# Unused tiles of 64 bytes between the pools of a spectral block with an MLP

## The chip, the cores and the metric

The kernel runs on one core of one Trainium2 chip. Times are device microseconds (us) of one execution. TensorE is the matmul engine, VectorE (DVE), ScalarE (ACT) and GpSimd (POOL) compute on tiles in SBUF, the on-chip memory of 128 partitions, and SyncE (SP) issues the DMAs. PSUM holds the results of matmuls. A matmul has two operands in SBUF: the weights, which a weight load brings into the array ahead of it (PEld in the profile), and the moving data, which stream through.

## The reference

One block with adaptive layer norm: a condition vector `c` gives six rows of scale, shift and gate; a spectral filter (a 2-D real FFT over 2048 x 512, a product with a complex weight, and back) is added to x, and then an MLP with Mish.

```
mod = (_silu(c) @ w_mod).reshape(c.shape[0], 6, 1, -1)
h = _layernorm(x) * (1 + ca) + sa
x = x + ga * irfft2(rfft2(h) * (w_r + 1j * w_i))
h = _layernorm(x) * (1 + cb) + sb
x = x + gb * (mish(h @ w1 + b1) @ w2)
```

x has 2048 rows of 512 float32 numbers, w1 is 512 x 1376, w2 1376 x 512.

## The kernel before, in words

The kernel runs in four stages, and in each the program's order is written out by hand, so the order in which an engine gets its work is the order of the calls.

The first stage goes over 16 groups of 128 rows. It does the FFT along the rows (line 206) and, as matrix products, along the columns (lines 251 to 253); the column matrices lie in `mring`, split into a high and a low part of type float32r, and the moving data in work buffers `g1` and `g2`. The second stage goes over 17 groups of frequencies: transpose (line 464), a small transform (line 485), the product with the filter on VectorE, transpose (line 518), a small transform back (line 531). The third goes back along columns (lines 666 and 667, with the matrices `kc`) and rows (line 676, with `kiv`) for the 16 groups. During it the weights w1 and the first parts of w2 are loaded and split.

The fourth is the MLP. It goes over 8 blocks of 256 rows, and in each over 6 items of the hidden dimension, item 0 with the 96 columns that are left over and items 1 to 5 with two tiles of 128. For an item, `up` multiplies by w1: four 512-wide matmuls with the high part `w1h` as weights and both parts of the MLP's input (`h2e` and `h2o`, for blocks of even and odd number) as moving data at line 755, then four 256-wide ones with the low part `w1l` at line 757, for each tile. ScalarE and VectorE make Mish of it (`front`, `back`) and sums of row halves, and `halves` splits the result into activations `ah` and `al` (lines 717 and 718). `down` takes these as weights and w2 as moving data: three passes (high by high, high by low, low by high) for each of seven products of half size, 21 matmuls of 256 columns in an item, at line 808. Item 0 (line 800) and parts of the last block (lines 820 and 823) have 512-wide matmuls instead. `down` of an item stands two items behind its `up`. All these matmuls are float32r, those of stages two and three and line 206 are float32.

Tiles come from pools that are set one behind another in SBUF: `base`, `small`, `work` (the nine work buffers), `big` (the tags `da`, `db`, `cr` and `ci`, each used by several tiles one after another: `mring` and then a part of w2 in `db`, `kc` and then `h2o` in `cr`), then `pw` and `hring` for the first two stages, and in their place `pm` (w1, w2, `h2e`) and `act` (the activations) for the others. A tile's first byte follows from the sizes of all tiles ahead of it. In the built program before, the work buffers, the tiles in `big`, w1, w2, `h2e` and the activations all begin 64 bytes past a multiple of 128; `kiv` begins 32 past one, and `modr` 96.

Of the kernel before, what the change touches and what calls it, by code (L numbers as in the profile page):

```python
# [7 lines left out]
F32 = mybir.dt.float32  # L8
# [4 lines left out]
P = 128  # L13
# [18 lines left out]
def tile_spectral_block(ctx: ExitStack, tc: tile.TileContext, x_d, w1_d, b1_d, w2_d,  # L32
# [4 lines left out]

    base = ctx.enter_context(tc.tile_pool(name="base", bufs=1))
    small = ctx.enter_context(tc.tile_pool(name="small", bufs=4))
    work = ctx.enter_context(tc.tile_pool(name="work", bufs=2))  # L40
    big = ctx.enter_context(tc.tile_pool(name="big", bufs=1))

    dram = ctx.enter_context(tc.tile_pool(name="dram", bufs=1, space=bass.MemoryType.DRAM))
# [555 lines left out]
        apply_gate()  # L599
    first.close()  # L600

    pm = ctx.enter_context(tc.tile_pool(name="pm", bufs=1))
    act = ctx.enter_context(tc.tile_pool(name="act", bufs=2))
    w1h = pm.tile([P, 4, F], F32R, name="w1h")
    w1l = pm.tile([P, 4, F], F32R, name="w1l")
    w2 = {}
    w2[1] = [pm.tile([P, 7, 256], F32R, name=f"w2{i}") for i in range(2)]
    w2hi = pm.tile([P, 7, 256], F32R, name="w2hi")
    w1v = w1_d.rearrange("(k p) f -> p k f", p=P)

    def piece(i):
# [495 lines left out]
```

## Time and profile before

| | us |
|---|---|
| median of 3 runs | 392.77 |
| lowest and highest run | 391.95, 393.06 |
| span of the profiled execution | 390.1 |
| of it TensorE busy | 383.2 |
| VectorE, ScalarE, GpSimd busy | 298.7, 247.3, 96.4 |
| stage of the MLP alone | from 165 on |

The span goes from the first to the last instruction of the profiled execution; what a run takes beside it is start and end. Matmuls overlap each other: the duration of one is longer than the time from its start to the start of the next, so the pace of a run of matmuls is read from starts, and busy time of TensorE near 100% says only that one followed another. PEld rows are weight loads, which run beside the matmul ahead of theirs. A row of a group gives line, engine, operation, tiles written and read, shapes and count, then busy time and mean duration in ns, then the idle time ahead. A row of the chain gives start, length and what ran. A row of waits gives who waited for whom, us in total, how often, and the longest.

### The profile page before, as it was taken

To read this page: it belongs to the slowest core of one execution; us is meant where nothing else is said; L and a number is where in the kernel's file an instruction comes from. 1 tells how busy PE (TensorE), PEld (TensorE's weight loads), DVE (VectorE), ACT (ScalarE), POOL (GpSimd) and SP (SyncE) were. 2 spreads that over 40 slices of the span, in tenths; PEclk is the share of its full clock that TensorE was granted. 3 is DMA by queue.
4 is the path that set the end of the run, shared out by engine and by line. 5 is a ranking of instruction groups with operands and counts; after the bars stand their busy time and mean duration, and the time that the engine had idled before them with its cause. 6 is when DMAs were issued, how large, how long until landed. Compare 5 with 4: busy or idle time off the path is not lost.

```text
span 390.1 us, 7373 instructions
## 1 busy us (share of the span) xinstructions
PE 383.2 (98%) x2744; PEld 355.3 (91%) x2744; DVE 298.7 (77%) x668; ACT 247.3 (63%) x545; POOL 96.4 (25%) x132
## 2 busy tenths in 40 slices
PE   8999999999999999999999999999999999999996
PEld 8899889999999998999999998999999999899984
DVE  1898978876299989887856965965966875987993
ACT  1788756678558647975855765674674674584750
POOL 0677736665077533300000000000000010017000
PEclk9999999999999999999999999999999999999999
DMA  8999994482143410100100100100100200122011
GB/s 262 376 296 343 311 361 141 134 315 55 55 114 87 145 49 28 56 3 0 55 0 3 54 2 0 56 0 2 55 2 0 76 0 2 50 61 106 3 54 54
DMA packets 21315, 36.70 MB, mean 94 GB/s; under 512 B 3840, under 2 KB 6752, under 8 KB 21024
## 3 DMA queue, kind: packets, MB, share of 16 engines
q1 hardware_dynamic: 21280, 36.24, 27.8%
q8 instruction: 21, 0.34, 0.4%
q14 instruction: 14, 0.11, 0.1%
HBM read 32.04 MB, written 4.20 MB: 93 GB/s over the span
## 4 chain that ended last, share of the span: by engine, by line
PE 89%; DVE 5%; ACT 4%; issue 1%; DMA 1%; SPq 0%; DVEq 0%; ACTq 0%
PE bank L808 24%; PE bank L755 20%; PE bank L757 10%; PE bank L485 3%; PE bank L531 3%; PE bank L676 3%; PE bank L206 3%; PE bank L251 3%; PE bank L666 3%; PE bank L667 3%; PE bank L800 2%; PE bank L820 2%; PE bank L645 2%; PE bank L464 2%; PE bank L518 1%; PE bank L262 1%
## 5 line engine op out<-in xcount | busy, mean ns | idle before, releaser
L765 ACT ACTIVATE buf<-bank,b1n 128x256 f32<-128x256 f32 (+1 forms) x88 | 40.8, 472 | 66.4 <-PE bank L757 66.1
L766 DVE TENSOR_TENSOR buf<-buf,bank 128x256 f32<-128x256 f32 (+1 forms) x88 | 35.3, 416 | 38.6 <-ACT buf L765 38.6
L718 DVE TENSOR_TENSOR al<-buf,ah 128x512 fp32r<-128x512 f32 (+2 forms) x85 | 53.7, 655 | 0.7 <-ACT ah L717 0.7
L737 POOL TENSOR_TENSOR buf<-buf,modr 128x512 f32<-128x512 f32 (+1 forms) x3 | 3.9, 1297 | 183.0 <-DMA buf<-in_B_w_dram 175.9
L755 PE MATMUL bank<-h2e,w1h 128*128 128x512 f32 (+1 forms) x176 | 48.4, 397 | 0.0
L755 PE MATMUL bank<-h2o,w1h 128*128 128x512 f32 (+1 forms) x176 | 48.3, 396 | 0.0
L717 ACT CAST ah<-buf 128x512 fp32r<-128x512 f32 (+2 forms) x85 | 43.0, 548 | 1.2 <-DVE buf L782 1.2
L782 DVE TENSOR_TENSOR buf<-buf 128x128 f32<-128x128 f32 x148 | 39.8, 310 | 3.5 <-ACT buf L772 2.2
L772 ACT ACTIVATE buf<-buf 128x512 f32<-128x512 f32 (+1 forms) x48 | 28.6, 596 | 15.3 <-DVE buf L766 15.2
L808 PE MATMUL bank<-w2a,ah 128*128 128x256 f32 x161 | 34.9, 286 | 0.0
L755 PEld LDWEIGHTS bank<-h2o,w1h 128*128 128x128 f32 (+1 forms) x176 | 30.2, 187 | 4.5
L755 PEld LDWEIGHTS bank<-h2e,w1h 128*128 128x128 f32 (+1 forms) x176 | 30.1, 187 | 4.5
L808 PE MATMUL bank<-w2b,ah 128*128 128x256 f32 x147 | 31.8, 283 | 0.0
L757 PEld LDWEIGHTS bank<-h2e,w1l 128*128 128x128 f32 (+1 forms) x176 | 26.7, 185 | 4.2
L757 PEld LDWEIGHTS bank<-h2o,w1l 128*128 128x128 f32 (+1 forms) x176 | 26.7, 185 | 4.2
L757 PE MATMUL bank<-h2e,w1l 128*128 128x256 f32 (+1 forms) x176 | 27.8, 280 | 0.0
L757 PE MATMUL bank<-h2o,w1l 128*128 128x256 f32 (+1 forms) x176 | 27.8, 280 | 0.0
L808 PEld LDWEIGHTS bank<-w2a,ah 128*128 128x128 f32 x161 | 26.7, 191 | 0.0
L667 PE MATMUL bank<-kc,d 128*128 128x128 f32 x128 | 24.8, 275 | 0.0
L666 PE MATMUL bank<-kc,d 128*128 128x128 f32 x128 | 24.7, 275 | 0.0
L808 PEld LDWEIGHTS bank<-w2b,ah 128*128 128x128 f32 x147 | 24.6, 191 | 0.0
L120 DVE BATCH_NORM_STATS2 st<-x 128x6 f32<-128x512 f32 x32 | 22.0, 688 | 0.4
(224 smaller groups left out, 1001.3 us busy)
## 6 DMA issues: line engine op xcount, KB each, us to landing
buf<-in_B_w_dram SPq DMA_DIRECT2D x20, 256.0 KB, 3.0
x<-in_A_x_dram SPq DMA_DIRECT2D x16, 256.0 KB, 5.1
xring<-in_x_t_dram SPq DMA_DIRECT2D x16, 256.0 KB, 5.1
wm<-in_w_mod_dram SPq DMA_DIRECT2D x16, 256.0 KB, 4.5
out_dram<-x SPq DMA_DIRECT2D x7, 512.0 KB, 2.6
mraw<-in_km_dram SPq DMA_DIRECT2D x16, 128.0 KB, 5.1
wqa<-in_w_q_dram SPq DMA_DIRECT2D x8, 256.0 KB, 4.3
wqb<-in_w_q_dram SPq DMA_DIRECT2D x8, 256.0 KB, 5.8
```

The costliest lines, as they stand in the source:

```text
L120: nc.vector.bn_stats(t, x[:, n, :])
L666: nc.tensor.matmul(o, dj[:, 0:128], kc[0][:, n, :], start=True, stop=False)
L667: nc.tensor.matmul(o, dj[:, 64:192], kc[1][:, n, :], start=False, stop=True)
L717: nc.scalar.copy(h, r)
L718: nc.vector.tensor_tensor(l, r, plain(h), op=ALU.subtract)
L755: nc.tensor.matmul(ps, w1h[:, k, fs], h[:, k], start=(k == 0), stop=False)
L757: nc.tensor.matmul(ps[:, 0:256], w1l[:, k, fs], h[:, k, 0], start=False, stop=(k == 3))
L765: nc.scalar.activation(o, ps[:, 256:], AF.Identity, bias=b1n[:rows, f:f + 1])
L766: nc.vector.tensor_tensor(o, o, ps[:, 0:256], op=ALU.add)
L772: nc.scalar.activation(o, o, AF.Mish)
L782: nc.vector.tensor_tensor(o, p, q, op=op)
L808: nc.tensor.matmul(o, a[p][:, e], w2[t][q][:, r], start=(own and half == 0 and t == 1 and i == 0), stop=(end and i == 2 and (n, half) != ( ...
```

## The change

A helper `shift` opens a pool with one tile of 16 float32 numbers a partition (64 bytes) that nothing writes or reads. It is called ahead of `work`, ahead of `big` and ahead of `pm`, and ahead of `act`, and one such tile stands in `pm` between w1 and w2. The pool `act` is opened after the tiles of `pm` are declared instead of ahead of them. Nothing else is changed: each engine has the same instructions in the same order with the same waits.

```diff
     base = ctx.enter_context(tc.tile_pool(name="base", bufs=1))
     small = ctx.enter_context(tc.tile_pool(name="small", bufs=4))
+
+    def shift(stack):
+        pool = stack.enter_context(tc.tile_pool(name="half_line", bufs=1))
+        pool.tile([P, 16], F32, name="half_line")
+
+    shift(ctx)
     work = ctx.enter_context(tc.tile_pool(name="work", bufs=2))
+    shift(ctx)
     big = ctx.enter_context(tc.tile_pool(name="big", bufs=1))
...
+    shift(ctx)
     pm = ctx.enter_context(tc.tile_pool(name="pm", bufs=1))
-    act = ctx.enter_context(tc.tile_pool(name="act", bufs=2))
     w1h = pm.tile([P, 4, F], F32R, name="w1h")
     w1l = pm.tile([P, 4, F], F32R, name="w1l")
+    pm.tile([P, 16], F32, name="half_line")
     w2 = {}
     w2[1] = [pm.tile([P, 7, 256], F32R, name=f"w2{i}") for i in range(2)]
     w2hi = pm.tile([P, 7, 256], F32R, name="w2hi")
+    shift(ctx)
+    act = ctx.enter_context(tc.tile_pool(name="act", bufs=2))
```

The first byte of the tiles that matter, in a partition, before and after, and what it leaves over a multiple of 128:

| tile | before | after |
|---|---|---|
| first work buffer | 51,520 (64) | 51,584 (0) |
| `mring`, later a part of w2 | 96,576 (64) | 96,704 (64) |
| `kc`, later `h2o` | 121,152 (64) | 121,280 (64) |
| `w1h`, `w1l` | 137,536, 159,552 (64) | 137,728, 159,744 (0) |
| first w2 in `pm` | 181,568 (64) | 181,824 (64) |
| `h2e` | 203,072 (64) | 203,328 (64) |
| `ah`, `al` (first) | 211,264, 218,432 (64) | 211,584, 218,752 (0) |

## The prediction

> **What bounds the kernel now.** The page's first part and its second come first, then the same busy times by stage.
>
> ```profile
> span 390.1 us, 7373 instructions
> PE 383.2 (98%) x2744; PEld 355.3 (91%) x2744; DVE 298.7 (77%) x668; ACT 247.3 (63%) x545; POOL 96.4 (25%) x132
> PEclk9999999999999999999999999999999999999999
> ```
>
> ```profile
> core 0: us, PE busy (x) PEld busy (x) DVE busy (x) ACT busy (x) POOL busy (x), PEclk, DMA share, GB/s
> ...
> 165.00:390.00 225.00, 221.29 (x1489) 202.71 (x1488) 168.19 (x383) 136.15 (x278) 10.66 (x9) 1.00 0.08 28
> ```
>
> TensorE is busy 98% of the span at the full granted clock. From 165 us on only the MLP is left, and there VectorE is busy 168.19 of 225 us, or 75%, ScalarE 61%, and the DMA engines 8%. A busy matmul row may hide waiting, so the next view is what the matmuls waited for. The longest waits of TensorE are these, and the rest are shorter:
>
> ```profile
> PE bank L292 <- DVE b1n L311: 1.1, 1, 1.1
> PE bank L262 <- DMA wmc<-in_w_mod_dram: 0.3, 1, 0.3
> ```
>
> So nothing feeds TensorE late; its own pace sets the end. The chain of waits gives that pace, because in the MLP it holds nothing but runs of matmuls, and each run's length is the time until the next run starts:
>
> ```profile
> 185.63 2.51 PE bank L808 x21
> 188.14 0.93 PE bank L755 x4
> 189.07 0.47 PE bank L757 x4
> 189.54 0.94 PE bank L755 x4
> 190.49 0.47 PE bank L757 x4
> 190.96 0.87 PE bank L645 x8
> 191.83 2.52 PE bank L808 x21
> ```
>
> A 256-wide matmul of line 808 starts every 2.51 us / 21 = 119.5 ns, a 512-wide one of line 755 every 0.93 / 4 to 0.94 / 4 = 234 ns, a 256-wide one of line 757 every 117 ns. These numbers come back block after block (2.51 or 2.52 us for the 21, whatever the other engines do), so what sets them lies in TensorE and in what it reads. The groups by form say the same in another unit: the duration of one matmul is a fixed tail longer than its pace.
>
> ```profile
> L755 PE MATMUL bank<-h2e,w1h 128*128 128x512 f32 x160 | 44.0, 396 | 0.0
> L808 PE MATMUL bank<-w2b,al 128*128 128x256 f32 x49 | 13.9, 283 | 0.0
> L757 PE MATMUL bank<-h2e,w1l 128*128 128x256 f32 x160 | 25.3, 280 | 0.0
> L820 PE MATMUL bank<-w2hi,al 128*128 128x512 f32 x4 | 1.6, 389 | 0.0
> L676 PE MATMUL bank<-kiv,buf 128*128 128x128 f32 x128 | 17.0, 276 | 0.1
> L531 PE MATMUL bank<-kv,buf 128*128 128x128 f32 x126 | 16.8, 276 | 0.2 <-ACT buf L521 0.2
> ```
>
> 283 - 119.5 and 396 - 234 and 280 - 117 all give about 163 ns of tail. With it every other row turns into a pace: line 820, also 512 wide, runs at 389 - 163 = 226 ns, 8 ns faster than line 755 with an equal shape; the float32 matmuls of 128 columns (lines 676 and 531) at 113 ns. Matmuls of one shape thus differ by 3 to 8 ns, always the same way at one place of the program, with no wait. They differ only in which tiles they read and in what went before. That the place in SBUF (the on-chip memory) of the two operands plays a part is a possible reading of this, not one that these rows prove.
>
> **The change part by part.** No engine gains, loses or reorders an instruction, and the same waits stand before the same instructions. The unused tiles hold no data and nobody writes them. What moves is where tiles lie. In the built program before, every tile that an MLP matmul reads, and the work buffers, start at 64 past a multiple of 128 bytes. After it the work buffers (51,520 becomes 51,584), w1h and w1l and the activations ah and al start at a multiple of 128; w2, h2e, h2o, the column matrices and the row matrices keep 64, since they move by 128 or 256. Weights and moving data of a matmul, before at equal place in the 128 bytes, now stand 64 apart at lines 251 to 253, 755, 757, 808, 800, 820 and 823, at 531, and at 485 for later groups. At 666 and 667 (both tiles in the same pool) and 676 (kiv starts at 32) less or nothing changes. So the change does what it says; the question is what the chip makes of it.
>
> The counts: line 808 has 21 matmuls in each of 37 items (7 blocks of 5, and 2 in the last), 777; lines 755 and 757 have 352 each, 251, 252 and 253 have 48 each; 800, 820 and 823 together 84.
>
> No row shows a float32r matmul (the single-pass kind of the MLP) whose operands stand 64 apart, so the cost of a place is bounded from both sides. *The good end.* A 256-wide matmul and a 128-wide float32 one each have a weight load of the same 128 columns to overlap, and the second runs at 113 ns, a price that the first may reach: 777 x 6.5 = 5.1 us at line 808, 352 x 4 = 1.4 us at line 757. If the 512-wide ones lose as much again below the quickest row, 226 - 6.5 = 219.5 ns, line 755 gives 352 x 14.5 = 5.1 us. The 48 of line 251 and the 84 of the last lines at some 10 ns give 1.3 us, lines 252 and 253 at 5 ns 0.5 us: 13.4 us together. *The bad end.* The nearest row for a weight load that the memory slows down is line 518, which takes its weights with a step of 16 bytes:
>
> ```profile
> L518 PEld LDWEIGHTS bank<-ident,buf 128*128 128x128 f32 x63 | 8.8, 205 | 0.0
> L531 PEld LDWEIGHTS bank<-kv,buf 128*128 128x128 f32 x126 | 15.5, 193 | 0.4 <-ACT buf L521 0.4
> L518 PE MATMUL bank<-ident,buf 128*128 128x128 f32 x63 | 10.1, 282 | 0.0
> ```
>
> Its load takes 12 ns more and its matmul 282 - 276 = 6 ns more than line 531. 6 ns on the 1,225 matmuls of 256 columns (777 + 352 + 96) is 7.4 us, and 5 ns on line 755 1.8 us: 9.2 us slower.
>
> *The value taken.* Between these ends I take the nearest rows of equal shape in this kernel: line 808 comes down to the pace of line 757 and line 755 to that of line 820, that is, each shape to a pace it already has somewhere. That is 777 x 3 = 2.3 us and 352 x 7 = 2.5 us; line 757 stays; line 251 as line 755, 48 x 7 = 0.3 us; 253 by 3 ns 0.1 us; the 48 of lines 800 and 823 by 6 ns 0.3 us. The sum is 5.5 us. All of it lies on the chain, because TensorE waits for nothing: the MLP's 225 us would become some 220, with VectorE at 168 / 220 = 76%, so nothing else takes over. Why a gain and not a loss: the paces that are to be explained lie above the quickest row of the same shape at nearly every place where all operands share one place in the 128 bytes, so there is more room below than above. This is a choice, not a proof.
>
> [...]
>
> *The float32 matmuls* of 128 columns (531, 485, 206) are costed at nothing: line 676, whose moving tile stands at 32, and line 531, where both stand at 64, have one duration, 276 ns, and loads of 192 to 193 ns. Were the shift worth 3 ns each way, the 126 and 72 of lines 531 and 485 would move the end by 0.6 us.
>
> *The other engines* read and write the moved buffers too. A change of some per cent there is hidden by the matmuls, which they wait for: ScalarE waits 66.1 us in all for line 757.
>
> ```profile
> ACT buf L765 <- PE bank L757: 66.1, 62, 2.2
> DVE buf L766 <- ACT buf L765: 38.6, 42, 2.3
> ```
>
> Where the cover is thin is the first stage, in which the DMA engines are 97% busy and line 251 shows mean durations of 434 instead of 398 ns; its DMA destinations move by 128 bytes only or not at all, so they keep their place in the 128.
>
> ```profile
> 0.00:46.00 46.00, 44.00 (x304) 40.79 (x305) 34.43 (x96) 30.66 (x72) 26.79 (x42) 1.00 0.97 324
> L251 PE MATMUL bank<-buf,mring 128*128 128x512 f32 x48 | 20.8, 434 | 0.6 <-ACT buf L237 0.3 <-DVE buf L244 0.2
> ```
>
> 1% more in these 46 us would be 0.5 us; I take nothing.
>
> The profiled execution has a span of 390.1 us; the median of the three runs is 392.77, so 2.7 us lie around the span. 390.1 - 5.5 = 384.6 us of span makes 387.3 us.
>
> **The rivals.** *First, the place does not matter* (no change, 392.8 us). For it speaks that lines 676 and 531 agree to the nanosecond although their operands stand differently, and that every 21 of line 808 take 2.51 us although their tiles lie in several places, all at 64. Against it, the spread within equal shapes needs some cause. [...]
>
> *Second, the whole excess goes*: the good end, 13.4 us, 392.8 - 13.4 = 379.4 us. For it: the change sets nearly every large matmul to the same new relation at once, so if the equal place is the one cause, all lines gain together. Against: line 820 is quick with all operands at 64.
>
> *Third, the new relation is the worse one* (slower). [...] Line 808's evenness, 119.5 ns at all 777, says its present relation is stable; line 755's steps over rows of 5,504 bytes, which mix places by multiples of 128, run slower than line 820 without such steps, so a relation other than the equal one can cost. Price: 3 ns on the 1,225 matmuls of 256 columns, 3.7 us, and 5 ns on the 352 of line 755, 1.8 us: 5.5 us, 398.3 us. It decides once the pace of line 808 rises above 120 ns.
>
> **How the numbers follow.** The forecast, 387.3 us with a range of its own of 383 to 391, has a chance of 0.35; the whole excess 0.2; no change 0.2; slower 0.25. A run of this kernel tells 0.3%, or 1.2 us, from no change. Faster by more is then 0.35 + 0.2 = 0.55, within it 0.2, slower 0.25. For the range, the low side reaches below the second rival, to 378 us, and leaves out what goes further (under 0.1); the high side reaches into the third, to 398 us, and leaves out its upper part (0.1).
>
> **What would show it.** Right: in the chain of waits the 21 matmuls of line 808 take 2.45 us (117 ns each) instead of 2.51, the 4 of line 755 0.91, with the number of instructions and TensorE's 98% unchanged. The whole excess: 2.37 us for the 21 and durations of 276 ns. No change: 2.51 and 0.93 to 0.94 again. Slower: 2.58 us or more for the 21. I would be wrong in kind if lines 808 and 755 moved in opposite directions, if the blocks of h2e and h2o (which now start differently to w1: 64 below and 64 above, modulo 512) had different paces, or if a new wait of TensorE appeared, by which the other engines and not the matmul's reads would carry the difference.

## The result and the profile after

The change is faster by less than forecast. The median of 4 runs is 389.87 us (389.21 to 390.44) beside 392.72 us of the kernel before in the same session; the ratio is 0.9927, with a 95% interval of 0.9907 to 0.9948, so 2.9 us, from 2.0 to 3.7. The forecast was 387.3 us, 5.5 us less than before. The profiled execution has a span of 387.8 us, 2.3 us less. The ratios here and below leave out slow executions, of which there was one: 1645.82 us among the first experiment's ten.

```profile
span 387.8 us, 7373 instructions
PE 380.7 (98%) x2744; PEld 353.1 (91%) x2744; DVE 298.9 (77%) x668; ACT 247.2 (64%) x545; POOL 96.3 (25%) x132
```

The instructions, TensorE's 98% and the other engines' busy times are as before. The longest waits of TensorE are these; the lines are numbered 7 to 10 higher than before (line 808 is now 818, 755 is 765, 820 is 830):

```profile
PE bank L299 <- DVE b1n L318: 1.1, 1, 1.1
PE bank L258 <- DVE buf L251: 0.9, 2, 0.7
PEld bank L765 <- DVE buf L776: 0.3, 1, 0.3
```

The first is as before. The second, in the first stage, was 0.2 us before, but it is 0.8 us also in the experiment below that moves the activations alone and leaves that stage as it was. The third is new: in the last block one weight load waits for VectorE, and the matmul behind it starts 0.31 us after the one ahead instead of some 0.23.

So the waits give no gain, and the gain is pace. In the chain of waits of the changed kernel, the same kind of stretch of the MLP that was shown of before:

```profile
185.29 2.48 PE bank L818 x21
187.77 0.93 PE bank L765 x4
188.70 0.47 PE bank L767 x4
189.17 0.93 PE bank L765 x4
190.11 0.48 PE bank L767 x4
190.59 0.87 PE bank L655 x8
191.46 2.48 PE bank L818 x21
193.94 0.91 PE bank L765 x4
```

21 matmuls of the down product take 2.48 us instead of 2.51 or 2.52 (118 ns each instead of 119.5), the four of the up product 0.91 to 0.93 instead of 0.93 to 0.94. The groups by form show the same, and that not every line gained:

```profile
L765 PE MATMUL bank<-h2e,w1h 128*128 128x512 f32 x160 | 43.5, 394 | 0.0
L818 PE MATMUL bank<-w2b,al 128*128 128x256 f32 x49 | 13.7, 280 | 0.0
L818 PEld LDWEIGHTS bank<-w2b,al 128*128 128x128 f32 x49 | 9.2, 188 | 0.0
L830 PE MATMUL bank<-w2hi,al 128*128 128x512 f32 x4 | 1.6, 395 | 0.0
```

Line 765 went from 396 to 394 ns and line 818 from 283 to 280, but the quick line of before, 820, went from 389 to 395 ns. A weight load of the down product is shorter too, 188 ns; before it was

```profile
L808 PEld LDWEIGHTS bank<-w2b,al 128*128 128x128 f32 x49 | 9.4, 192 | 0.0
```

Since both programs have the same matmuls in the same order, the time from each start to the next can be summed by line. Line 808 went from 93.5 to 91.8 us (1.7 us less), 755 from 82.5 to 81.5 (1.0 less), 757 stayed at 41.5 and 41.4, 800 and 820 together went from 18.4 to 18.7 (0.3 more, 0.08 of it the new wait). In the float32 lines 485, 531, 666, 667 and 676 the sums agree to 0.02 us.

The first three stages are one source of noise. The first matmul of line 755 starts, before and after, at

```profile
142.46 1.16 PE L755 MATMUL bank<-h2e,w1h 128*96 128x512 f32 x4
```

```profile
142.68 1.16 PE L765 MATMUL bank<-h2e,w1h 128*96 128x512 f32 x4
```

and in the experiments anywhere from 141.4 to 143.7 us, also where these stages are unchanged. From that start to the end of the span it is 390.1 - 142.5 = 247.6 us before and 387.8 - 142.7 = 245.1 us after. This length, called the MLP's length below, carries the comparisons by single profiles.

### The profile page after: what moved, and what is told of

Same layout as the page of the kernel before. It is cut to its first block, busy times and chain, and to the rows that moved or that the text cites. A ratio compares the mean times of both kernels' runs of the same rounds, so it can differ in the third digit from the quotient of the medians.

```text
span 387.8 us, 7373 instructions
## 1 busy us (share of the span) xinstructions
PE 380.7 (98%) x2744; PEld 353.1 (91%) x2744; DVE 298.9 (77%) x668; ACT 247.2 (64%) x545; POOL 96.3 (25%) x132
## 4 chain that ended last, share of the span: by engine, by line
PE 84%; DVE 5%; DMA 4%; ACT 4%; issue 1%; SPq 0%; DVEq 0%; ACTq 0%
PE bank L818 24%; PE bank L765 20%; PE bank L767 10%; PE bank L492 3%; PE bank L538 3%; PE bank L686 3%; PE bank L677 3%; PE bank L676 3%; PE bank L810 2%; PE bank L830 2%; DMA modr<-scb 2%; PE bank L655 2%; PE bank L471 2%; PE bank L258 2%; PE bank L525 1%
```

## The experiments

Two theories had to be told apart first: that a matmul's pace hangs on how its two operands stand to each other (R), or on where a tile begins by itself (A). In all diffs below, `pad(ctx, n)` opens a pool with one unused tile of n bytes a partition. All are edits of the kernel before, and in all that use `pad` the pool `act` is opened after the tiles of `pm`, as in the change. Runs with no ratio are single executions.

**Both operands moved alike.** One unused tile of 64 bytes ahead of the work buffers, and none after it.

```diff
+    pad(ctx, 64)
     work = ctx.enter_context(tc.tile_pool(name="work", bufs=2))
```

> One unused tile of 64 bytes ahead of the work buffers and none after it: all tiles from there on begin at a multiple of 128 bytes, so weights and moving data stand to each other exactly as before, only the place of both is moved by 64. Theory R (the relation of a matmul's two operands sets the pace): nothing changes, 2.51 us for the 21 matmuls of line 808's run, 0.93 to 0.94 us for the 4 of line 755, 392.7 us in all, within 1. Theory A (a tile that begins at a multiple of 128 is read faster by itself): as the change or better, 2.48 us, 0.92 us, 390 us or less.

Measured: 391.45 us, a ratio of 0.9991 (0.9969 to 1.0013) to before. The MLP's length is 389.3 - 141.7 = 247.6 us, as before, and the chain has the old times:

```profile
191.11 2.51 PE bank L817 x21
193.62 0.93 PE bank L764 x4
194.55 0.47 PE bank L766 x4
195.02 0.94 PE bank L764 x4
```

Where a tile begins by itself changed nothing here. Theory A is out.

**The places exchanged.** Weights at 64 past a multiple of 128, moving data at a multiple of it.

```diff
     work = ctx.enter_context(tc.tile_pool(name="work", bufs=2))
+    pad(ctx, 64)
...
+    pad(ctx, 64)
     pm = ctx.enter_context(tc.tile_pool(name="pm", bufs=1))
...
     w1l = pm.tile([P, 4, F], F32R, name="w1l")
+    pm.tile([P, 16], F32, name="pad")
...
+    pad(ctx, 64)
+    act = ctx.enter_context(tc.tile_pool(name="act", bufs=2))
```

> The change with its places exchanged: work buffers, w1 and activations 64 past a multiple of 128 as before, and w2, the MLP's input and the column matrices at a multiple of 128. Theory R (relation): as the change, 2.47 to 2.48 us for the 21 matmuls of the MLP's down product, 0.92 us for the 4 of the up product, 390 us within 1. Theory A (the weights' own place at a multiple of 128 counts): as before, 2.51 us and 0.93 to 0.94 us, 392.7 us.

Measured: 390.38 us, a ratio of 0.9953 (0.9931 to 0.9975); 2.47 to 2.48 us for the 21 of most items, 0.92 to 0.93 us for the 4, an MLP's length of 388.9 - 143.7 = 245.2 us. That is the change's gain in the MLP (245.1 us) with the places exchanged: it is the relation that counted.

**The activations alone.**

```diff
+    pad(ctx, 64)
+    act = ctx.enter_context(tc.tile_pool(name="act", bufs=2))
```

> Only the activations are moved by 64 bytes, everything else stays as before. If each line's pace hangs on its own two operands: the 21 of the down product in 2.48 us, the 4 of the up product still in 0.93 to 0.94 us, the 512-wide matmuls with activations as weights slower by some 5 ns as in the change, a span of 390.1 - 1.5 = 388.6 us. If the gain came from the work buffers or from w1 through other engines: nothing at the down product, 390.1 us.

Measured: a span of 390.1 us, but with a late start of the MLP; its length is 390.1 - 143.5 = 246.6 us, 1.0 less than before. The chain has the expected times, 2.48 us for the 21, whose operands were moved against each other, and 0.93 to 0.94 us for the 4, whose operands were not:

```profile
192.68 2.48 PE bank L817 x21
195.16 0.93 PE bank L764 x4
196.09 0.47 PE bank L766 x4
196.56 0.94 PE bank L764 x4
```

The span was a miss, 390.1 us for 388.6 expected: the MLP starts 1.0 us later, and it gained 1.0 us instead of 1.5. The 512-wide matmuls with activations as weights lost 6 ns, about as expected: at line 820 the median time from start to start is 227 ns before and 233 here.

**A sweep of the distance.** Work buffers, w1 and activations are moved by n bytes, and a second unused tile after the first two brings all else back to its old place modulo 512. With n = 64 this differs from the change in one thing: in the change, padding adds up so that the activations stand 64 from some w2 tiles and 192 from others (modulo 256), and w1 192 from `h2e` and 64 from `h2o`.

```diff
+    pad(ctx, n)
     work = ctx.enter_context(tc.tile_pool(name="work", bufs=2))
+    pad(ctx, 512 - n)
...
+    pad(ctx, n)
     pm = ctx.enter_context(tc.tile_pool(name="pm", bufs=1))
...
     w1l = pm.tile([P, 4, F], F32R, name="w1l")
+    pm.tile([P, (512 - n) // 4], F32, name="pad")
...
+    pad(ctx, n)
+    act = ctx.enter_context(tc.tile_pool(name="act", bufs=2))
```

> Work buffers, w1 and activations are moved by 64 bytes and every other tile keeps its place modulo 512, so that all pairs stand exactly 64 apart modulo 512; in the change some stand 192 or 64 the other way. If only the place modulo 128 counts: the lines as in the change, 2.47 to 2.48 us for 21 and 0.92 to 0.93 us for 4, a span of 387.8 us within 0.7. If the place modulo 512 counts: other paces than in the change, by 1 ns a matmul or more, above all at those products whose distance differs (w2 in the large tiles).

> The sweep by 64 once more, now timed. If its 113.3 ns a matmul of the down product is what its places give each time: 387.7 us within 0.7, 1.1% under before. If it was the luck of one execution: 113.3 ns in the profile again or not, and a median of 390 us.

> As the sweep by 64, with 128 bytes instead: operands that stood at equal place now stand 128 apart modulo 512. Theory B (only the place modulo 128 counts, two alternating halves of 64 bytes): everything as before, 2.51 us for the 21 of the down product (119.5 ns each), 0.93 to 0.94 us for the 4 of the up product, a span of 390 us within 0.7. Theory M (a longer period): another pace, by 1 ns a matmul or more.

> As the sweep by 64, with 256 bytes: theory B as before, 119.5 ns a matmul of the down product and a span of 390 us within 0.7; theory M another pace.

> As the sweep by 64, with 32 bytes, so that half of each 64-byte piece overlaps. Theory B: between before and the sweep by 64, 113 to 120 ns for a matmul of the down product. Theory M: no statement but that it differs from 119.5 ns.

> As the sweep by 64, with 192 bytes, the distance at which the change puts the activations and the large w2 tiles. If only the place modulo 256 and the footing from the matmuls ahead decide: down products at 113.3 or 117.8 ns a matmul, run by run, and none at 119.5; a span of 386 to 389 us. If 192 is one more kind of place with its own pace, as 128 was (117, 120, 123 ns in turn): another figure in all runs.

| n | 21 of the down product, us | one of them, ns | MLP's length, us |
|---|---|---|---|
| 0 (before) | 2.51 to 2.52 | 119.5 to 120 | 247.6 |
| 32 | 2.48 to 2.50 | 118 | 246.6 |
| 64 | 2.38 to 2.40, but for one of 2.48 and two with a wait inside | 113.3 | 242.5 and 242.3 |
| 128 | 2.49 to 2.52 | 118.5 to 120 | 247.5 |
| 192 | 2.38 or 2.47 | 113.3 or 118 | 243.7 |
| 256 | 2.51 to 2.52 | 119.5 to 120 | 247.9 |

256 gives the paces of 0 again, run for run. 128 does not, although its span, 390.2 us, and its MLP are as long as before: summed by line, 755 takes 81.59 us instead of 82.50, and 757 takes 42.15 instead of 41.48. A group of line 757 (now 767) at 128 and at 256, where it has its old 280 ns:

```profile
L767 PE MATMUL bank<-h2e,w1l 128*128 128x256 f32 x160 | 25.7, 283 | 0.0
...
L767 PE MATMUL bank<-h2e,w1l 128*128 128x256 f32 x160 | 25.3, 280 | 0.0
```

So of the shifts that were run, the one by 256 bytes repeats the paces of none, twice the period that the change was drawn for. At 64 nearly all of the down product falls to 113.3 ns, a pace that no line of its shape kept before (117 to 119.5 ns):

```profile
191.34 2.40 PE bank L818 x21
193.74 0.92 PE bank L765 x4
194.66 0.47 PE bank L767 x4
```

Timed, n = 64 has a median of 386.56 us, quicker than the 387.7 within 0.7 that was expected, and a ratio of 0.9859 (0.9838 to 0.9881) to before. It beats both kernels: the change's interval, 0.9907 to 0.9948, lies above it. At 192 the runs alternate between two paces, 2.38 and 2.47, in one kernel; its span of 385.1 us is below the 386 to 389 expected, since its MLP starts at 141.4:

```profile
190.02 2.38 PE bank L818 x21
...
195.20 2.47 PE bank L818 x21
...
199.06 2.38 PE bank L818 x21
...
204.23 2.47 PE bank L818 x21
```

**Is it the weight load?** The kernel before, with the down product's weights read at one address.

```diff
-                nc.tensor.matmul(o, a[p][:, e], w2[t][q][:, r], ...
+                nc.tensor.matmul(o, a[p][:, e, 0:1].to_broadcast([P, P]), w2[t][q][:, r], ...
```

> The kernel before, with the weights of the 21 down products of an item read as one column of the activations, repeated 128 times: the weight load has the same length and reads one address over and over; the products themselves are other ones, so the MLP's result is not computed. Theory C (the weight load's walk through SBUF collides with the walk of the moving data): the pace leaves 119.5 ns, down to 113 ns or less. Theory F (a float32r matmul has a fixed overhead of 13 ns): 119.5 ns stays, 2.51 us for the 21.

Measured: nothing is moved, yet the 21 take 2.38 to 2.41 us, and the MLP's length is 385.7 - 142.8 = 242.9 us.

```profile
L808 PE MATMUL bank<-w2b,al 128*128 128x256 f32 x49 | 13.5, 276 | 0.0
L808 PEld LDWEIGHTS bank<-w2b,al 128*128 128x128 f32 x49 | 9.2, 188 | 0.0
```

The load still has its 128 columns, and 188 ns (192 before). With one address read in place of 128 columns, the down product's matmuls go from 283 to 276 ns. Theory F's 13 ns are what the paces of lines 808 and 820 before leave as a constant part (2 x 119.5 - 226); 6 to 7 of them are gone here, so as a fixed overhead those are out. Theory C's pace came; that two reads collide is its reading, and no trace shows a collision. (The load brings other values, too, and no run changes the values alone; but the sweep by 64 reaches the same pace, 113.3 ns, with the values unchanged.) Lines 755 and 757 fall as well, from 82.5 to 81.8 us and from 41.5 to 41.3, though their own operands are read as before: here the pace of a line changed with that of its neighbours. What sets the 113.3 ns that are left is open.

**What chooses between 113.3 and 118 ns?** With the activations alone moved, every run of 21 had 118; with work buffers and w1 moved too, 113.3, though the down product's operands stand alike in both. So w1 and the activations were moved without the work buffers (shown against the sweep by 64):

```diff
-    pad(ctx, n)                        # n = 64, around the work buffers
-    pad(ctx, 512 - n)
```

> As the sweep by 64, but the work buffers stay where they are before: w1 and the activations are moved by 64 bytes, all else keeps its place modulo 512. With the activations alone moved, the down product ran at 117.8 ns, with work buffers and w1 moved as well at 113.3. If the matmuls that run ahead (the up product) set the footing on which the two streams start: 113.3 ns, a span of 385.6 us within 0.7. If the work buffers do it, through the engines that read and write them beside TensorE: 117.8 ns, 388.5 us.

Measured: both, and a span of 386.1 us. The MLP's length is 386.1 - 143.1 = 243.0 us.

```profile
185.55 2.38 PE bank L818 x21
...
190.71 0.87 PE bank L655 x8
191.58 2.48 PE bank L818 x21
...
196.86 2.40 PE bank L818 x21
```

Runs that follow the up product have 2.38 to 2.40 us, but for one of 2.53 with a wait inside; the one in each block that follows the transposes of line 655 has 2.47 or 2.48. Those transposes take work buffers as weights, and with the work buffers moved as well they lead, but for one case, into the quick pace (2.40 us, above). So at a distance of 64 or 192 two steady paces occur, 113.3 and 118 ns, and in this layout the one that a run has goes with what ran ahead of it.

It does not settle it alone. The sweep by 64 was profiled in two executions of one program, and the run behind the first block's transposes took, in the one and in the other,

```profile
161.97 2.48 PE bank L818 x21
...
161.90 2.40 PE bank L818 x21
```

Nor does a run always keep its pace. In the first of these executions a weight load in the last block waits,

```profile
360.09 0.30 PEld L818 LDWEIGHTS bank<-w,ah 128*128 128x128 f32 x2 [0.29 <-DVE modr L854]
```

and the matmuls of that run start every 113 ns ahead of the wait and every 118 ns behind it; in the other execution the same load waits 0.16 us, and the pace is 113 ns on both sides. Program and tiles are the same; what made the difference between the two executions is not shown. The change itself has both paces: 4 of its 37 runs of 21 take 2.38 to 2.40 us, the others 2.47 or 2.48.

**A layout drawn by this reading.** The sweep by 64 with w1's rows padded, so that the up product's steps over rows no longer mix distances.

```diff
-    w1h = pm.tile([P, 4, F], F32R, name="w1h")
-    w1l = pm.tile([P, 4, F], F32R, name="w1l")
+    w1h = pm.tile([P, 4, 1408], F32R, name="w1h")
+    pm.tile([P, 16], F32, name="pad1")
+    w1l = pm.tile([P, 4, 1408], F32R, name="w1l")
...
-            w2[0] = [w[:, 5376:5888], w2["lo"]]
+            w2[0] = [w[:, 5392:5904], w2["lo"]]
```

> The sweep by 64 with the rows of w1 padded from 5,504 to 5,632 bytes, so that all four steps of the up product stand alike modulo 256; the high part of w1 at equal place with the MLP's input, the low part 64 apart; w2's last part of 96 rows moved by 64, to equal place with the activations. If the place modulo 256 of one matmul's load and stream sets its pace, with 226.7 ns for 512 columns at equal place and 113.3 ns for 256 columns at 64 apart: line 755 goes to 226.7 ns (from 230, 1.1 us in all), line 757 to 113.3 ns (from 116, 0.9 us), the 512-wide matmuls of item 0 from 232 to 227 ns (0.2 us), 385.5 us within 1. If the footing of the matmuls ahead decides as much as the place: one of these stays off, and the down product may fall back to 117.8 ns, 389 us.

Measured: 390.2 us, a ratio of 0.9941 (0.9923 to 0.996), worse than the sweep by 64. The second expectation held in kind. Summed by line, 755 takes 81.8 us (81.35 in the sweep) and 757 41.6 (41.1); only the 512-wide matmuls of item 0 gained, 0.1 us instead of the 0.2 expected. And most runs of the down product fell back:

```profile
186.11 2.48 PE bank L819 x21
...
192.26 2.40 PE bank L819 x21
...
197.45 2.48 PE bank L819 x21
...
201.33 2.39 PE bank L819 x21
```

Modulo 256 the down product's distances are the sweep's, whose runs took 2.38 to 2.40 us, but for the few in the table: the distance alone did not set the pace.

## Why the prediction came out as it did

**What bounds the kernel** held: TensorE's 98% stayed, and the gain that the profiles show, 2.5 us, is pace in the MLP. One new wait appeared, for VectorE in the last block, of the kind that the prediction names among its signs of being wrong; at 0.08 us it carries none of the gain.

**The choice of a gain** held, and the runs show what the prediction called a possible reading, that the place of the two operands in SBUF plays a part: with the places exchanged the 21 take 2.47 to 2.48 us, with both moved alike 2.51, and with one column as the weights, and nothing moved, 2.38 to 2.41. How the weight load and the moving data bear on each other, no run shows. The reason given for a gain, that most places lay above the quickest row, named no cause, and at 128 the same kind of move gains nothing (an MLP of 247.5 us beside 247.6).

**The sum was too large**, 5.5 us for 2.9 measured, and its terms fail one by one. Line 808 was priced at 3 ns, to the pace of line 757; it came to 1.7 us / 777 = 2.2 ns (the paces that the prediction reads from the chain, 119.5 and 117, would have made it 2.5), and the sign of being right, 2.45 us for the 21, was not reached. That it came so near is luck: the new distance gives 113.3 or 118 ns, and nothing in the prediction chose between them. Line 755 was priced at 7 ns, to the pace of line 820, 2.5 us; it gained 1.0 us / 352 = 2.8 ns. This is the step that failed most. Line 820 was quick with its operands at equal place, which the change took away: it went from 389 to 395 ns. A row with the old relation was used as the price of the new one, although the prediction itself noted that fact against its second rival. The old relation would not have brought line 755 there either: with padded rows, all its steps at equal place, it took 81.8 us / 352 = 232 ns, not 226. The 0.3 us of gain put at lines 800 and 823 became, with 820, 0.3 us of loss. Lines 251 and 253, priced at 7 and 3 ns, moved by 1 ns each (medians of 235 and 234, and of 119 and 118, from start to start).

The 2.7 us put around the span were 0.6 too many: the four executions of the changed kernel last 2.0 to 2.1 us longer than their spans.

**The float32 matmuls at nothing** held to 0.02 us a line. (What the prediction calls single-pass has one record for each matmul in the trace, 777 for line 808's 777, where the float32 line 531 has two for each of its 63.) **The other engines** were not seen to slow a steady run, the 21 of line 808 taking 2.51 or 2.52 us in the chain whatever they did; but with the same instructions on TensorE and only the tiles moved, a 256-wide matmul went from 119.5 to 113.3 ns, 6.2 ns less, in the sweep by 64.

**The rivals.** "The place does not matter" fell. "The whole excess goes" was not this change's result, but most of line 808's part of it was to be had: the priced pace was 113 ns, the sweep by 64 shows 113.3. "The new relation is the worse one" was right at the lines where it was not looked for, 800 and 820, and wrong at line 808, where it was; no run shows its prices of 3 and 5 ns at lines 808 and 755, which went down by 2.2 and 2.8 ns instead. Of the other signs of a wrong kind, lines 808 and 755 did not part, and blocks of `h2e` and `h2o` did not differ at line 765 (394 ns in both groups); but the changed kernel's three runs of 2.38 us all stand in blocks of even number, those of `h2e`.

## What to carry to other kernels

Where TensorE is the bound, compare the pace of matmuls of one shape at different lines; a spread without a wait (here 117 to 119.5 ns for 256 columns) changed in this case with where weights and moving data stand to each other, and unused bytes between pools test that in one run. Take a price for a new relation only from a row that already has it, not from one that is quick under the old. Read each line's pace again after any change of layout, since here line 820 went from 389 to 395 ns where line 808 went from 283 to 280, and with work buffers unmoved the runs behind the transposes had 2.47 or 2.48 us where the others had 2.38 to 2.40.

## What the runs showed of the hardware that was not expected

A shift by 256 bytes repeats the paces of none (2.51 to 2.52 us for the 21), and one by 128, the period that the change was drawn for, does not (line 757 takes 42.15 us instead of 41.48). At distances of 64 and 192 a run of equal matmuls has two steady paces, 113.3 and 118 ns, and mostly keeps the one it starts in; in one run it went from 113 to 118 ns behind a wait of 0.29 us, and two executions of one program differed in it (2.48 and 2.40 us). Only float32r matmuls showed the effect; for the float32 ones of lines 485 and 531, with a weight load of the same 128 columns, the median time from start to start is 112 ns before and after, and the group of line 531 has a mean duration of 276 ns at shifts of 0, 32, 64, 128, 192 and 256 alike. Why the distance counts, what picks one of the two paces and why the pace ends at 113.3 ns, no run here shows.
